# Turning q ahead of the last x tile, finishing its scalings a block earlier, and moving one tile's numerators behind a pair's second product

## The chip, the cores and the metric

The kernel runs on one core of one Trainium2 chip. The core's engines work side by side, each through its own list of instructions in a fixed order, and wait for one another through semaphores: PE (TensorE, matrix products; its weight loads are listed as PEld), DVE (VectorE), ACT (ScalarE), POOL (GpSimd) and SP (SyncE, which here only issues transfers; "SPq" in the profile is its queue). Transfers run on the core's 16 DMA engines. The metric is the device time of one execution in microseconds, less being better; several executions of each kernel are timed, and one more is recorded by the hardware profiler.

## The reference: what is computed

A linear attention (cosformer) over 8 batches, 8 heads, 576 positions and head size 64, and behind it a feed-forward block with a GELU gate over the 8·576 = 4608 tokens.

```python
theta = np.pi / 2.0 * pos / S
phi = lambda x: np.concatenate([np.maximum(x, 0) * cos_w, np.maximum(x, 0) * sin_w], axis=-1)
q_p, k_p = phi(q), phi(k)
kv  = np.einsum('bhsf,bhsd->bhfd', k_p, v)
z   = np.sum(k_p, axis=2)
num = np.einsum('bhsf,bhfd->bhsd', q_p, kv)
den = np.einsum('bhsf,bhf->bhs', q_p, z)[..., None] + 1e-06
attn_out = num / den                       # (8, 8, 576, 64)
x = attn_out.transpose(0, 2, 1, 3).reshape(4608, 512)
g = x @ w_gate                             # (4608, 1536)
gelu = 0.5 * g * (1.0 + erf(g / sqrt(2)))
out = (gelu * (x @ w_val)) @ w_out         # (4608, 512)
```

## The kernel before, in words

**Two sizes of work.** Attention goes by batch b (576 tokens, five tiles t = 0 to 4 of 128 tokens, the last one half used). The feed-forward part goes by block n of 512 tokens, nine blocks. The order of the instructions on every engine is the order of the Python calls; nothing is moved by a scheduler. While block n's feed-forward work runs, the attention of batch n+1 is made in between. The change touches blocks 3, 4 and 5.

**Attention of a batch.** q and k, staged in float32 (tile st), are scaled by cosine and sine tables and clipped at zero: `prep_both(b, part, j, engine)` does this for q and k together for one of nine position groups j, on ACT (line 192; "s8" is the sine part of group 8, "c8" the cosine part). When all 18 scalings of a batch are done, `turn_q(b)` issues two DMA transposes on SP (line 223, phis to qT). The tile qT has one buffer for all batches. `kv_unit(b)` makes the 72 small products of k and v (line 271). `nm_unit(b, t)` makes the numerators and denominators of one tile: eight products of qT with kv (line 312) into the PSUM banks 6 and 7, then three DVE instructions (lines 323 to 325: add, reciprocal, multiply) that leave x_sb. `turn_x(b, t)` turns x_sb into xT by one or two DMA transposes on SP (line 379); xT is what the feed-forward products read. x_sb has four buffers.

**Feed-forward from block 3 on.** The gate and value products of a pair of 128-wide column groups are made by seven half-size products instead of eight (class `Pair`, line 655, methods p1 to p7), with sums of weights made beforehand and sums of xT made by `x_sum` on POOL (line 635, T1 to T4 into tile fs). In blocks 3 to 5 there are five pairs for the column groups 0 to 9, and groups 10 and 11 are done by the plain `gv_unit` (line 431), one inside the third pair, one inside the fifth. The output products (line 548, `product`) are those of the block before, spread over the slots; their sums of hT are made on POOL (line 530) and their results collected on DVE (lines 561 and 566).

**The order.** `step(new, old, a, b, c)` interleaves one pair with attention: p1, p5, `a()`, p6, p2, `b()`, p3, and, where a plain unit follows, p7, the unit with `c()` in the middle, p4. a, b and c are slots: `slot(n, jt)` runs `o_step` (output products of block n-1, every third time a `flush` that puts stores on SP), then `attention(n, jt)`, then `more(n, jt)` (the x_sums of block n+1 are in slots 8 to 11). A pair's p7 and p4 are otherwise left to the pair behind it ("old"). The pairs of blocks 3 to 5 take the slots (0, 1), (2, 3), (4, 5, 6), (7, 8) and (9, 10, 11); the first and the fourth have no old pair. `numerators(n, jt)` decides by slot number which tile is made: the table in it maps a slot to a tile of batch n+1 (slot 0: the last tile of batch n). In the fourth pair it is called behind p1.

**Two waits inside a pair** matter here. p2 adds onto a copy of p1 that ACT makes (line 674); p3 adds onto bank MIX, which p6's DVE instruction writes (line 682), so PE cannot begin p3 before line 682 has ended on DVE, and DVE takes line 682 only behind the collecting of the output products of slot `a()` (lines 566 and 561).

**`attention(n, jt)`** first turns the x tiles whose numerators have been made since the last slot, then (slot 0, blocks 4 to 6) does the last two scalings s8 and c8 of batch n+1, then (slot 0, in block 3 slot 1) `turn_q(n+1)`, then `start_loads` (the loads of a later batch's q, k and v, on SP), then `kv_unit` in slot 1, and `preps` (the scalings of batch n+2 by the table PREPS).

Of the kernel before, what the change touches and what calls it, by code (L numbers as in the profile page):

```python
# [16 lines left out]
def kernel(  # L17
# [13 lines left out]
    nc = tc.nc  # L31
# [8 lines left out]
    R = S // 64  # L40
# [54 lines left out]
    def load(eng, name, b, m0, m1, j0=0, j1=R):  # L95
        if (name, b) not in staged:
            staged[name, b] = stage(name, b)
        eng.dma_start(
            out=staged[name, b][:, m0:m1, j0 * D:j1 * D],
            in_=rows(srcs[name], b)[:, m0:m1, j0 * D:j1 * D],  # L100
        )
# [64 lines left out]
    def phi_tile(name, b):  # L166
        phi[name, b] = phis[:, 1 if name == "k" else 2 * (b % 2) * (b > 2)]
        return phi[name, b]
# [15 lines left out]
    def prep_both(b, part, j, eng):  # L184
        for name in "qk":
            phi_tile(name, b)
        o = phis[:, b % 2:b % 2 + 2, :, j, part * D:(part + 1) * D]
        o = o.rearrange("p a m d -> p (a m) d")
        i = st[:, 0:2, :, j * D:(j + 1) * D].rearrange("p a m d -> p (a m) d")
        tab = (cos_t, sin_t)[part]  # L190
        if eng is nc.scalar:
            nc.scalar.activation(o, i, AF.Relu, scale=tab[:, j:j + 1])  # L192
        else:
            eng.tensor_scalar(o, i, 0.0, tab[:, j:j + 1], op0=ALU.max, op1=ALU.mult)  # L194
# [26 lines left out]
    def turn_q(b):  # L221
        for i in range(2):
            nc.sync.dma_start_transpose(
                out=qt_tile(b)[:, i].rearrange("f m (j p) -> f (m j) p", p=64),
                in_=phi["q", b][64 * i:64 * i + 64].rearrange("p m j f -> p (m j f)"),
            )
# [83 lines left out]
    def nm_unit(b, t, b0=6):  # L310
        for h in range(H):
            nc.tensor.matmul(  # L312
                bank(b0 + h // 4)[:, (h % 4) * (D + 1):(h % 4 + 1) * (D + 1)],
                lhsT=q_cols(b, t, h),
                rhs=kv_sb[b][:, h // 2, h % 2, :],
                start=True,
                stop=True,
            )
        nm = ps[:, b0:b0 + 2, 0:4 * (D + 1)].rearrange("p g (h d) -> p g h d", h=4)
        den = attn2.tile([128, 2, 4], FP32, name="den")  # L320
        rec = attn2.tile([128, 2, 4], FP32, name="rec")
        x = xsp.tile([128, 2, 4, D], BF16, name="x_sb")
        nc.vector.tensor_scalar_add(den, nm[:, :, :, D], EPS)
        nc.vector.reciprocal(rec, den)
        nc.vector.tensor_tensor(  # L325
            x,
            nm[:, :, :, 0:D],
            rec[:, :, :, None].to_broadcast([128, 2, 4, D]),
            op=ALU.mult,
        )  # L330
        xs[b, t] = x.rearrange("p g h d -> p (g h d)")
# [30 lines left out]
    def xT_block(blk):  # L362
        if blk not in xT:
            xT[blk] = xtp.tile([128, CT, BLK], BF16, name="xT")
        return xT[blk]

    def pieces(b, t):

        o = max(128 * (t + 1) - S, 0)
        c0, n = b * S + t * 128, 128 - o  # L370
        while n > 0:
            m = min(n, BLK - c0 % BLK)
            yield c0 // BLK, c0 % BLK, o, m
            c0, o, n = c0 + m, o + m, n - m

    def turn_x(b, t):
        x = xs.pop((b, t))
        for blk, c, o, m in pieces(b, t):
            nc.sync.dma_start_transpose(
                out=xT_block(blk)[:, :, c:c + m], in_=x[o:o + m, :]  # L380
            )
# [39 lines left out]
    def gv_unit(n, jt, c0=0, w=BLK, to=None, between=None):  # L421
        xt = xT[n]
        js = slice(jt * 128, (jt + 1) * 128)
        if to is None:
            to = (0, 1) if turn[0] % 2 == 0 else (2, 3)
            turn[0] += 1
        if n not in hT:
            hT[n] = ffn.tile([128, JT, BLK], BF16, name="hT")
        for g, wt in ((0, wg_sb), (1, wv_sb)):
            for ct in range(CT):  # L430
                nc.tensor.matmul(  # L431
                    bank(to[g])[:, 0:w],
                    lhsT=wt[:, ct, js],
                    rhs=xt[:, ct, c0:c0 + w],
                    start=(ct == 0),
                    stop=(ct == CT - 1),
                )
            if g == 0:
                gel = ffn.tile([128, BLK], FP32, name="gel")
                nc.scalar.activation(gel[:, 0:w], bank(to[0])[:, 0:w], AF.Gelu)  # L440
                if between:
                    between()
        nc.vector.tensor_mul(  # L443
            hT[n][:, jt, c0:c0 + w], gel[:, 0:w], bank(to[1])[:, 0:w]
        )
# [168 lines left out]
    def w_sum(name, j0, j1, eng=nc.vector):  # L614
        x, y, op = {
            "S1": ("A21", "A22", ALU.add),
            "S2": ("S1", "A11", ALU.subtract),
            "S3": ("A11", "A21", ALU.subtract),
            "S4": ("A12", "S2", ALU.subtract),
        }[name]  # L620
        eng.tensor_tensor(w_part(name, j0, j1), w_part(x, j0, j1), w_part(y, j0, j1), op=op)
# [83 lines left out]
    def step(new, old, a, b, c=None, std=None, to=None):  # L705

        n, (jt, *_) = new.n, new.at
        new.p1()
        if old:
            old.p7(6)  # L710
        elif n < 6:
            numerators(n, jt)
        new.p5()
        a()
        new.p6()
        if old:
            old.p4()
        new.p2()
        if n < 6 and old:
            numerators(n, jt + 1)  # L720
        b()
        new.p3()
        if std:
            new.p7(MIX)
            preps(n, f"m{std}")

            def between():
                numerators(n, jt + 2)
                c()
                new.p4()  # L730

            gv_unit(n, std, to=(to, to), between=between)
# [206 lines left out]
    def start_loads(n, jt):  # L939
        for b, name, *part in LOADS.get((n, jt), ()):  # L940
            if len(part) == 1:
                load(nc.sync, name, b, part[0], part[0] + 2)
            elif part:
                load(nc.sync, name, b, 0, NP, *part)
            else:
                for m in (0, 2):
                    load(nc.sync, name, b, m, m + 2)
# [63 lines left out]
    def early(jt):  # L1011
        for what in EARLY.get(jt, "").split():
            part = "cs".index(what[0])
            prep_both(4, part, int(what[1]), nc.scalar if part or jt > 8 else nc.gpsimd)

    def block2():
# [37 lines left out]

    PREPS = {
        2: "s0 c0", 4: "s1 c1", 5: "s2", "m10": "c2", 6: "s3 c3", 7: "s4 c4",
        9: "s5 c5", 10: "s6", "m11": "c6", 11: "s7 c7",
    }
    turns = []

    def preps(n, jt):
        b = n + 1
        if 3 < b < B - 1:
            for what in PREPS.get(jt, "").split():
                prep_both(b + 1, "cs".index(what[0]), int(what[1]), nc.scalar)

    def numerators(n, jt):
        b, t = n + 1, {6: 0, 7: 1, 10: 2, 11: 3, 0: 4}.get(jt)
        if jt == 0:
            b = n  # L1070
        if t is not None and b > 3:
            nm_unit(b, t)
            turns.append((b, t))

    def attention(n, jt):
        made = list(turns)
        if n > 5:
            if (n, jt) == (6, 0):
                numerators(n, jt)
            i, b = n * JT + jt - 6 * JT - 7, B - 1  # L1080
            if i in (0, 2, 4, 6, 8):
                nm_unit(b, i // 2)
                turns.append((b, i // 2))
        for bt in made:
            turn_x(*bt)
            turns.remove(bt)
        b = n + 1
        if (n, jt) == (3, 0):
            early(JT)
        elif jt == 0 and n < 7:  # L1090
            prep_both(n + 1, 1, R - 1, nc.scalar)
            prep_both(n + 1, 0, R - 1, nc.scalar)
        if n == 3 and 2 < jt < 7:
            w_sum(("S1", "S2", "S4", "S3")[jt - 3], WJ, WX, eng=nc.gpsimd)
        if jt == (n == 3) and b < B:
            turn_q(b)
        start_loads(n, jt)
        if b >= B:
            return
        if jt == 1:  # L1100
            kv_unit(b)
        preps(n, jt)
        if b + 1 < B and jt in (7, 8):
            m = 2 * (jt - 7)
            cast_v(b + 1, m, m + 2, nc.gpsimd.tensor_copy)
# [14 lines left out]
    old, places = None, (0, 1, 2)  # L1120
    for n in range(3, NB):
        jt = 0
        for T in range(JT // 2):
# [7 lines left out]
            jt = jts.stop  # L1131
            old, places = (None, (other, at, to)) if std else (new, (to, other, at))
# [55 lines left out]
```

## Time and profile before

| what | value |
|---|---|
| median of 3 runs | 308.31 us (308.21 to 309.02) |
| the profiled execution | 307.53 us, of which the span (first to last instruction) is 305.7 us |
| PE busy | 295.3 us, 97% of the span |
| PE weight loads | 228.8 us, 75% |
| DVE, ACT, POOL busy | 74%, 66%, 54% |
| granted TensorE clock | 0.996 of full speed |
| SP's transfers (queue q1) | 41.17 MB, 61.4% of the 16 DMA engines' span |
| blocks 3, 4 and 5 | 112.6 to 143.6, 143.6 to 175.3 and 175.3 to 205.9 us (from the first output product of each to that of the next) |

How to read it: an engine's busy share tells how little idle time there is to win; the timeline of PE shows where that idle time lies, as the distance between the end of one group of products and the start of the next; the chain of waits names what released PE at such a place; and the timeline of SP shows when each transfer was issued, since its queue takes them strictly one behind the other. Starts in a timeline are microseconds from the start of the span. Consecutive products overlap in the records, so the distance from start to start of the groups is what counts.

### The profile page before, as it was taken

To read this page: it belongs to the slowest core of one execution; us is meant where nothing else is said; L and a number is where in the kernel's file an instruction comes from. 1 tells how busy PE (TensorE), PEld (TensorE's weight loads), DVE (VectorE), ACT (ScalarE), POOL (GpSimd) and SP (SyncE) were. 2 spreads that over 40 slices of the span, in tenths; PEclk is the share of its full clock that TensorE was granted. 3 is DMA by queue.
4 is the path that set the end of the run, shared out by engine and by line. 5 is a ranking of instruction groups with operands and counts; after the bars stand their busy time and mean duration, and the time that the engine had idled before them with its cause. 6 is when DMAs were issued, how large, how long until landed. Compare 5 with 4: busy or idle time off the path is not lost.

```text
span 305.7 us, 8024 instructions
## 1 busy us (share of the span) xinstructions
PE 295.3 (97%) x3089; PEld 228.8 (75%) x3107; DVE 227.5 (74%) x496; ACT 202.1 (66%) x399; POOL 163.8 (54%) x140
## 2 busy tenths in 40 slices
PE   7899999999999999999999999999999999999993
PEld 3574456745786668787878788888898988888882
DVE  5866995998995765879676967796678785766772
ACT  7865592997572797878685878686655556555630
POOL 6585430000000989976935594579935965397310
PEclk9999999999999999999999999999999999999998
DMA  7999999989999989997799889937833521303045
GB/s 264 257 172 211 343 292 389 303 169 226 204 152 211 346 241 157 218 300 199 113 214 277 205 131 155 319 60 132 134 75 63 60 46 34 71 0 73 0 88 122
DMA packets 73175, 53.68 MB, mean 176 GB/s; under 512 B 45392, under 2 KB 62544, under 8 KB 73136
## 3 DMA queue, kind: packets, MB, share of 16 engines
q1 hardware_dynamic: 63360, 41.17, 61.4%
q0 software_dynamic: 9696, 11.93, 17.0%
q8 instruction: 24, 0.39, 0.5%
q14 instruction: 15, 0.12, 0.1%
q10 hardware_dynamic: 80, 0.07, 0.1%
HBM read 37.75 MB, written 9.44 MB: 154 GB/s over the span
## 4 chain that ended last, share of the span: by engine, by line
PE 77%; DMA 7%; DVE 6%; issue 5%; POOL 1%; ACT 1%; SPq 1%; POOLq 0%; DVEq 0%
PE ps L655 29%; PE ps L548 19%; PE ps L431 18%; PE ps L464 3%; PE ps L312 3%; DMA qT<-phis 3%; PE ps L271 3%; DMA st<-in_v_dram 2%; DMA wv_sb<-in_moe_w_val_dram 2%; DVE hT L443 1%; DVE phis L180 1%; POOL st L530 1%; PE ps L402 1%; PE ps L234 1%; DVE ps L682 1%
## 5 line engine op out<-in xcount | busy, mean ns | idle before, releaser
L530 POOL TENSOR_TENSOR sm<-hT 128x768 bf16<-128x768 bf16 x24 | 39.4, 1640 | 21.0 <-PE ps L655 8.0
L695 DVE TENSOR_TENSOR ps<-fs,ps 128x512 f32<-128x512 f32 x33 | 22.9, 695 | 27.7 <-PE ps L655 26.1
L431 PE MATMUL ps<-xT,wg_sb 128*128 128x512 bf16 (+1 forms) x172 | 41.3, 349 | 0.6
L431 PE MATMUL ps<-xT,wv_sb 128*128 128x512 bf16 (+1 forms) x182 | 41.8, 351 | 0.1
L655 PE MATMUL ps<-fs,ws 128*128 128x256 bf16 x288 | 40.8, 273 | 0.0
L655 PEld LDWEIGHTS <-ws 128*128 128x128 bf16 x384 | 36.3, 98 | 5.7 <-issue 0.7
L655 PE MATMUL ps<-xT,wg_sb 128*128 128x256 bf16 x264 | 39.6, 272 | 0.0
L194 POOL TENSOR_SCALAR phis<-st,cos_t 128x512 bf16<-128x512 f32 x4 | 7.9, 1984 | 54.8 <-PE ps L312 54.8
L443 DVE TENSOR_TENSOR hT<-gel,ps 128x512 bf16<-128x512 f32 (+1 forms) x46 | 28.0, 614 | 11.3 <-PE ps L431 8.6
L548 PEld LDWEIGHTS <-sm 128*128 128x128 bf16 x336 | 32.5, 98 | 4.5
L440 ACT ACTIVATE gel<-ps 128x512 f32<-128x512 f32 (+1 forms) x46 | 24.6, 541 | 15.8 <-PE ps L431 14.5
L548 PEld LDWEIGHTS <-hT 128*128 128x128 bf16 x288 | 28.0, 98 | 4.0 <-issue 0.2
L561 DVE TENSOR_TENSOR o_sb<-sm,ps 128x256 f32<-128x256 f32 x56 | 23.4, 417 | 10.1 <-ACT sm L566 8.9
L687 ACT ACTIVATE gel<-ps 128x512 f32<-128x512 f32 x33 | 19.6, 593 | 16.8 <-PE ps L655 16.7
L678 ACT COPY fs<-ps 128x512 f32<-128x512 f32 x33 | 19.3, 586 | 16.4 <-DVE ps L695 15.3
L655 PEld LDWEIGHTS <-wg_sb 128*128 128x128 bf16 x264 | 25.8, 98 | 4.7
L431 PEld LDWEIGHTS <-wv_sb 128*128 128x128 bf16 x184 | 17.9, 98 | 15.2 <-issue 0.3
L325 DVE TENSOR_TENSOR x_sb<-ps,rec 128x512 bf16<-128x512 f32 x38 | 26.3, 691 | 1.3
L530 POOL TENSOR_TENSOR sm<-hT,sm 128x768 bf16<-128x768 bf16 x12 | 19.7, 1639 | 11.9 <-PE ps L548 7.0
L192 ACT ACTIVATE phis<-st,sin_t 128x512 bf16<-128x512 f32 x36 | 25.7, 719 | 0.0
L431 PEld LDWEIGHTS <-wg_sb 128*128 128x128 bf16 x184 | 17.0, 98 | 11.4
L696 DVE TENSOR_TENSOR hT<-gel,ps 128x512 bf16<-128x512 f32 x33 | 22.7, 688 | 3.2
(134 smaller groups left out, 634.6 us busy)
## 6 DMA issues: line engine op xcount, KB each, us to landing
out_dram<-o_sb SPq DMA_DIRECT2D x69, 128.0 KB, 3.1
st<-in_v_dram SPq DMA_DIRECT2D x10, 576.0 KB, 7.5
st<-in_q_dram SPq DMA_DIRECT2D x5, 640.0 KB, 5.4
st<-in_q_dram SPq DMA_DIRECT2D x5, 512.0 KB, 5.7
st<-in_k_dram SPq DMA_DIRECT2D x4, 640.0 KB, 6.9
st<-in_k_dram SPq DMA_DIRECT2D x4, 576.0 KB, 4.6
st<-in_q_dram POOLq DMA_DIRECT2D x4, 576.0 KB, 12.0
st<-in_k_dram SPq DMA_DIRECT2D x4, 512.0 KB, 5.2
```

The costliest lines, as they stand in the source:

```text
L192: nc.scalar.activation(o, i, AF.Relu, scale=tab[:, j:j + 1])
L325: nc.vector.tensor_tensor(x, nm[:, :, :, 0:D], rec[:, :, :, None].to_broadcast([128, 2, 4, D]), op=ALU.mult,)
L431: nc.tensor.matmul(bank(to[g])[:, 0:w], lhsT=wt[:, ct, js], rhs=xt[:, ct, c0:c0 + w], start=(ct == 0), stop=(ct == CT - 1),)
L440: nc.scalar.activation(gel[:, 0:w], bank(to[0])[:, 0:w], AF.Gelu)
L443: nc.vector.tensor_mul(hT[n][:, jt, c0:c0 + w], gel[:, 0:w], bank(to[1])[:, 0:w])
L530: eng.tensor_tensor(a[name][:, j0:j1], a[x][:, j0:j1], a[y][:, j0:j1], op=op)
L548: nc.tensor.matmul(at, lhsT=hs.setdefault(key, h_parts(n, p))[a][:, j], rhs=ts[b][:, j], start=(j == 0 and i in ((1, 2, 4, 5), (1, 4, 5))[ ...
L561: nc.vector.tensor_tensor(o, got[key, k], x, op=op)
L655: nc.tensor.matmul(to[:, 256 * half:256 * half + 256], lhsT=w_part(a, j * 128, (j + 1) * 128)[:, ct], rhs=xb[self.n][b][:, ct], start=(hal ...
L687: nc.scalar.activation(self.gel0, self.other, AF.Gelu)
L695: nc.vector.tensor_tensor(bank(val), self.m5, self.sum, op=ALU.add)
L696: nc.vector.tensor_tensor(self.h(1), both(gel1), both(bank(val)), op=ALU.mult)
```

## The change

It has three parts, all in blocks 3 to 5 and the slots next to them. The numerators of tile 1 move, in the fourth pair, from behind p1 (slot number 7) to behind p2 (slot number 8); with them goes their turn_x, from slot 7 to slot 8, behind that slot's flush on SP. The scalings s8 and c8 of batches 5, 6 and 7 move from slot 0 of blocks 4, 5 and 6 to slot 11 of the blocks ahead, behind s7 and c7 on ACT. And in the slot of turn_q, turn_q and the loads that go with it are issued ahead of the x tile that was made since the last slot (tile 4 of batches 4 and 5), where they were issued behind it. No work is added or left out.

```diff
@@ step
         if old:
             old.p4()
         new.p2()
-        if n < 6 and old:
+        if n < 6:
             numerators(n, jt + 1)
         b()
         new.p3()
@@ PREPS
         2: "s0 c0", 4: "s1 c1", 5: "s2", "m10": "c2", 6: "s3 c3", 7: "s4 c4",
-        9: "s5 c5", 10: "s6", "m11": "c6", 11: "s7 c7",
+        9: "s5 c5", 10: "s6", "m11": "c6", 11: "s7 c7 s8 c8",
     }
@@ numerators
     def numerators(n, jt):
-        b, t = n + 1, {6: 0, 7: 1, 10: 2, 11: 3, 0: 4}.get(jt)
+        b, t = n + 1, {6: 0, 8: 1, 10: 2, 11: 3, 0: 4}.get(jt)
         if jt == 0:
             b = n
@@ attention
-        for bt in made:
-            turn_x(*bt)
-            turns.remove(bt)
         b = n + 1
         if (n, jt) == (3, 0):
             early(JT)
-        elif jt == 0 and n < 7:
-            prep_both(n + 1, 1, R - 1, nc.scalar)
-            prep_both(n + 1, 0, R - 1, nc.scalar)
         if n == 3 and 2 < jt < 7:
             w_sum(("S1", "S2", "S4", "S3")[jt - 3], WJ, WX, eng=nc.gpsimd)
         if jt == (n == 3) and b < B:
             turn_q(b)
-        start_loads(n, jt)
+            start_loads(n, jt)
+        for bt in made:
+            turn_x(*bt)
+            turns.remove(bt)
+        if jt != (n == 3):
+            start_loads(n, jt)
         if b >= B:
             return
```

## Prediction

> **What bounds the kernel now.** I read the page first: PE is busy 97% of the span, so only idle time of PE can be won, and no part of the change alters what PE computes. PE's list of waits over the whole span names one wait in blocks 3 to 5, and the chain of waits through block 4 (start us, length us, what) shows where it lies and a second place that the list does not name (first row the page's, the second that of the waits, then the chain):
>
> ```profile
> PE 295.3 (97%) x3089; PEld 228.8 (75%) x3107; DVE 227.5 (74%) x496; ACT 202.1 (66%) x399; POOL 163.8 (54%) x140
> ...
> PE ps L312 <- DMA qT<-phis: 0.7, 1, 0.7
> ...
> 150.51 8.54 DMA qT<-phis
> ...
> 159.10 0.40 PE ps L312 x7
> ...
> 163.93 0.43 DVE sm L566
> ...
> 164.73 0.70 DVE ps L682
> 165.43 0.04 issue
> 165.47 1.91 PE ps L655 x16
> ```
>
> So PE hung on the second transpose of q (line 223), and 6 us later on line 682. How long it stood is read from PE's timeline of block 4, start to start:
>
> ```profile
> 157.38 1.03 PE L431 MATMUL ps<-xT,wg_sb 128*128 128x512 bf16 x3
> 158.24 0.19 PE L312 MATMUL ps<-kv_sb,qT 128*128 128x65 bf16 x1
> 159.10 0.40 PE L312 MATMUL ps<-kv_sb,qT 128*128 128x65 bf16 x7 [0.67 <-DMA qT<-phis]
> 159.33 0.82 PE L548 MATMUL ps<-wo_sb,sm 128*128 128x256 bf16 x6
> ...
> 164.60 0.82 PE L548 MATMUL ps<-wo_sb,sm 128*128 128x256 bf16 x6
> 165.47 0.60 PE L655 MATMUL ps<-xT,ws 128*128 128x256 bf16 x4
> ```
>
> From line 431 to line 548 it is 159.33 − 157.38 = 1.95 us; the same stretch is 127.64 − 126.51 = 1.13 in block 3 and 190.20 − 189.07 = 1.13 in block 5. The wait for q costs 0.82 us, once. From that pair's second batch of output products to p3 it is 0.87, where six such products otherwise take 0.66: 0.21 us lost, and the same 0.87 stands in block 3 (132.90 to 133.77) and block 5 (195.46 to 196.33). SP's timeline shows why q came late: it issued two x transposes, then q without a pause, then the loads. The third row is the x tiles 0 and 1, the fourth the x_sum that waits for them:
>
> ```profile
> 144.02 2.58 SPq L379 DMA_TRANSPOSE xT<-x_sb  x2
> 146.71 7.90 SPq L223 DMA_TRANSPOSE qT<-phis  x2
> 154.66 1.60 SPq L98 DMA_DIRECT2D st<-in_q_dram  x1
> ...
> 161.47 4.36 SPq L379 DMA_TRANSPOSE xT<-x_sb  x3
> ...
> 167.79 1.16 POOL L635 TENSOR_TENSOR fs<-xT 128x512 bf16<-128x512 bf16 x1 [1.11 <-DMA xT<-x_sb]
> ```
>
> **Part 1, q ahead of the x tile (blocks 4 and 5), with s8 and c8 a slot earlier.** SP has turn_q issued at 146.71 because tile 4's transpose (half of 2.58: 1.29 us) is ahead of it. Without that, it can go at 144.02 + 1.29 = 145.31 if c8 is done. c8 began at 145.08 on ACT and would have ended at 145.8; in slot 11 it comes behind c7. ACT starts one scaling each 0.61 us: s7 140.82, c7 141.44, so s8 142.05, c8 142.66, ending 143.37. The last readers of the one qT buffer, tile 4's products, start at 142.78 and are over at 143.2. So q leaves 1.40 us earlier, bounded by its issue on SP. It landed at 159.05, 12.34 us after its first issue; the same 12.34 from 145.31 gives 157.65, and PE asks at 158.24. The wait goes with 0.59 us to spare: −0.82 us. Bounds: 0 (landing not moved) and −0.82. In block 5 q does not hold PE, so the same move is worth nothing there; in block 6 only c8 is earlier, also nothing.
>
> What the earlier scalings are put ahead of: ACT's copy of p1 (line 674), which began at 143.50 after 1.35 us of idle time waiting for DVE line 700. ACT is free again at 142.66 + 0.61 = 143.27, so it is not late; the same holds at 175.20 (1.36 idle) and 206.06 (1.35), for 2 × 0.61 = 1.22. If it were late by 0.2 us, p2 would hide it: it starts at 144.57, 0.5 us behind the copy's end. 0, bounds 0 and +0.1 a block.
>
> What q and the loads are put ahead of: tile 4's transpose, then four stores (158.97). SP's own order is only permuted, so from the stores on it stands where it stood. Tile 4 leaves at about 157.6 instead of 145.3, behind seven transfers. Its first reader is the x_sum at 167.79. The longest any x transpose took to land is 7.6 us (median 3.7): 165.2, before that. x_sb has four buffers, and tile 4's is written next as tile 3 of the next batch at 173.5. Hidden by some 2.6 us: 0. The loads go 1.4 us earlier into stages whose last readers are the moved scalings: 0.
>
> **Part 2, tile 1's numerators behind p2 (blocks 3, 4, 5).** The eight products take PE 0.26 us wherever they stand. Taken from behind p1 and put behind p2, they let p5, the output products of slot 7, p6 and p2 begin 0.26 earlier, and the output products of slot 8 begin when they did. DVE line 566 begins 0.02 us after the output products (163.91 in the chain), so lines 566, 561 and 682 follow them 0.26 earlier: 682 ends at 165.17 instead of 165.43. PE is ready for p3 at 164.60 + 0.66 = 165.26. The 0.21 us go, with 0.05 left; next late is PE itself. 3 × −0.21 = −0.63. Bounds −0.63 and 0: if line 561 or p6's products bound line 682 and not line 566, nothing is won.
>
> The three DVE instructions (0.20, 0.24 and 0.60 us from start to start: 1.04) leave the place ahead of line 566, where DVE then waited 0.62, and go behind line 682, ahead of line 695, where DVE waited 1.56 (166.98 in block 4). They fit: 165.07 to 166.3. Line 695 writes bank 6, which they read, and starts behind them anyway. 0.
>
> Behind them hangs tile 1's turn_x: x_sb ends at 166.3 instead of 163.3, and slot 8's two stores (1.22 us) now go ahead of it, into the time in which SP waits. In block 4 the tile is two transposes, issued at 166.35 and 167.55. X transposes issued around there landed in 3.4 to 5.9 us, median 4.3: 171.9. POOL, with 3.37 us idle before its next work, then makes T1 to T4, 1.24 and 3 × 1.11 us: T1 is there at 173.1, T2 at 174.2. Block 5 reads T1 in p5 at 174.74 − 0.21 = 174.53 and T2 in p6 at 175.62. Spare: 1.4 us. In block 3 it is one transpose: x_sb 134.5, landed 139.1 at that stretch's median of 4.5, T1 at 140.2, needed at 142.83; spare 2.6. Block 6 does not read batch 6's tile 1 at all. So 0, bounds 0 and +2.3 (third rival).
>
> **Where the trace and the Trainium skill differ.** The two q transposes move 2 × 590 kB (64 rows of 4608 two-byte values each) in 12.34 us: 96 GB/s. The Trainium skill ("DMA: Bandwidth & Descriptors", section "Latency and other measured facts") gives 261 GB/s as measured for DMA transposes in one kernel. By that figure, as an estimate, both would be through in 4.5 us, q would never have held PE, and only the 0.63 us would be left to win (307.7). The trace shows the wait, so the sum goes by the trace.
>
> **Sum.** −0.82 − 0.63 = −1.45, less a residue of 0.02 to 0.05 a block in part 2: −1.4 us. The profiled execution took 307.53 us (span 305.7), so 306.1 for one like it; it lay 0.78 below the median of the runs, so I forecast 308.31 − 1.4 = **306.9 us**, 0.45% less.
>
> **The rivals.**
> 1. The landing of q does not move. It is bound by what the DMA engines already carry (their share is 0.92 at 144 to 146 us and about 1 from 148 on), not by SP's issue. Against it: the share is 0.26 at 146 to 148, so q found them idle. The time: −0.63 alone, 307.7.
> 2. Line 682 does not come earlier, because p6's products or line 561 bound it. For it: the chain has 0.30 us of "issue" between lines 561 and 682. Against: that is pipelining on DVE, whose start spacing is the same everywhere. The time: −0.82 alone, 307.5. Both together: no change, 308.3.
> 3. The later x tile ends on the other side. Place: the first x_sum in slot 8 of blocks 3 and 4, and p5 of the next block's first pair behind it. It decides from a landing of 5.7 us in block 4 on. At the longest landing of the trace, 7.6 us from an issue at 167.55, T1 is there at 175.15 + 1.2 = 176.35 and PE waits 1.8 us; in block 3 134.55 + 7.6 + 1.2 = 143.35, 0.5 us. With the gains: −1.4 + 2.3 = +0.9, 309.2. For it: the stores now ahead of it, and landings that vary threefold. Against: the loads of block 4 are by then 1.4 us further on, and the landings beside them are below 6.
>
> **How the numbers follow.** A measurement of this kernel can tell about 0.3%, 0.9 us. Forecast 0.68 (its own range 306.3 to 307.4); rival 1 0.10, rival 2 0.09, both together 0.04, rival 3 0.09. The forecast lies 1.4 below and counts as faster, rivals 1 and 2 (0.6 and 0.8 below) mostly as same, with some of each as faster because the runs' own spread (0.8) reaches over the line, rival 3 as slower or same. Faster 0.74, same 0.18, slower 0.08. The range takes in rivals 1 and 2 and leaves out no change and rival 3: 306.2 to 308.0.
>
> **What would show it.** In the changed profile: no wait of PE line 312 for qT, and line 431 to line 548 at 1.13 in block 4; q's transposes issued directly behind one x transpose; 0.66 to 0.70 in place of 0.87 ahead of p3 in all three blocks; line 566 to 682 unchanged in spacing, lines 323 to 325 between 682 and 695; POOL's first line 635 of blocks 3 and 4 two to three us later, and no gap of PE at the first pair of blocks 4 and 5. The prediction is wrong if such a gap appears there, if q still lands after PE asks, or if ACT's line 674 starts late at the block's edge.

## The result, and the profile after

| | before | changed |
|---|---|---|
| median of 12 runs | 308.36 us | 306.14 us |
| lowest and highest | 307.29 to 309.94 | 305.41 to 308.49 |
| the profiled execution, and its span | 307.53, 305.7 | 305.74, 304.0 |

The ratio of the runs is 0.9927, with a 95% interval of 0.9905 to 0.9950: the change is worth 2.2 us (1.5 to 2.9). I had forecast 1.4 us, in a range from 306.2 to 308.0. The direction was right, the size too small, and the time lies 0.06 us below the range.

Of the two profiled executions alone, the forecast held. This is PE's timeline of the changed kernel in block 4 and at its two edges (start, length, engine, line, operands, count):

```profile
145.95 1.33 PE L271 MATMUL ps<-vx,phis 64*128 64x65 bf16 x72
...
156.91 1.03 PE L431 MATMUL ps<-xT,wg_sb 128*128 128x512 bf16 x3
157.78 0.42 PE L312 MATMUL ps<-kv_sb,qT 128*128 128x65 bf16 x8
158.03 0.82 PE L548 MATMUL ps<-wo_sb,sm 128*128 128x256 bf16 x6
...
163.04 0.42 PE L312 MATMUL ps<-kv_sb,qT 128*128 128x65 bf16 x8
163.30 0.82 PE L548 MATMUL ps<-wo_sb,sm 128*128 128x256 bf16 x6
163.96 0.60 PE L655 MATMUL ps<-xT,ws 128*128 128x256 bf16 x4
...
176.60 1.33 PE L271 MATMUL ps<-vx,phis 64*128 64x65 bf16 x72
```

From line 431 to line 548 it is now 1.12 us (1.95 before), so the wait for q is gone; from the second output products to p3 it is 0.66 (0.87 before), and 0.66 and 0.65 in blocks 3 and 5. From one block's products of k and v (line 271) to the next it is 30.65, 30.65 and 30.64 us, against 30.86, 31.71 and 30.85: 0.21, 1.06 and 0.21, together 1.48. That is the forecast's sum of 1.45, and nothing has come in its place. The other 0.25 us of the 1.7 by which the spans differ had arisen before block 3 (line 271 there at 115.30 and 115.55), where the two kernels are the same.

SP's timeline of the changed kernel, and below it ACT's, show the moved steps as forecast: q directly behind one x transpose, the loads behind it, then the last x tile; and c8 (ACT's first row) before the copy of p1 (line 674), which starts 2.91 us ahead of line 271 in both kernels:

```profile
143.56 1.28 SPq L379 DMA_TRANSPOSE xT<-x_sb  x1
144.95 8.04 SPq L223 DMA_TRANSPOSE qT<-phis  x2
153.03 1.44 SPq L98 DMA_DIRECT2D st<-in_q_dram  x1
...
157.08 1.20 SPq L379 DMA_TRANSPOSE xT<-x_sb  x1
```

```profile
142.20 0.71 ACT L192 ACTIVATE phis<-st,cos_t 128x512 bf16<-128x512 f32 x1
143.04 0.57 ACT L674 COPY ps<-ps 128x512 f32<-128x512 f32 x1
```

So the open question was not what the change does, but why the runs gave 2.2 us where one profile of each kernel adds up to 1.5. Theory A: the excess is the spread of the runs. Theory B: the wait for q varies from execution to execution, and the one profile of before that I had read caught a short one.

### The profile page after: what moved, and what is told of

Its sections match the earlier page's. It is cut to its first block, busy times and chain, and to the rows that moved or that the text cites. A ratio compares the mean times of both kernels' runs of the same rounds, so it can differ in the third digit from the quotient of the medians.

```text
span 304.0 us, 8032 instructions
## 1 busy us (share of the span) xinstructions
PE 294.7 (97%) x3089; PEld 228.8 (75%) x3107; DVE 226.7 (75%) x496; ACT 202.2 (67%) x399; POOL 165.9 (55%) x140
## 4 chain that ended last, share of the span: by engine, by line
PE 75%; DMA 8%; issue 5%; DVE 4%; POOL 3%; ACT 2%; SPq 1%; POOLq 0%; DVEq 0%; ACTq 0%
PE ps L655 32%; PE ps L548 19%; PE ps L431 14%; DMA st<-in_v_dram 5%; PE ps L464 3%; PE ps L271 3%; PE ps L312 2%; DMA wv_sb<-in_moe_w_val_dram 2%; DVE hT L443 2%; SPq L98 1%; POOL st L530 1%; DMA xT<-x_sb 1%; ACT phis L178 1%; PE ps L402 1%; POOL fs L635 1%
## 5 line engine op out<-in xcount | busy, mean ns | idle before, releaser
L443 DVE TENSOR_TENSOR hT<-gel,ps 128x512 bf16<-128x512 f32 (+1 forms) x46 | 28.0, 613 | 11.5 <-PE ps L431 8.8
## 6 DMA issues: line engine op xcount, KB each, us to landing
st<-in_q_dram POOLq DMA_DIRECT2D x4, 576.0 KB, 12.1
```

Of the source, the lines that this page charges most:

```text
L443: nc.vector.tensor_mul(hT[n][:, jt, c0:c0 + w], gel[:, 0:w], bank(to[1])[:, 0:w])
```

## The experiments

**The kernel before, again, and the changed kernel, again** (no edit).

> The kernel before, unchanged, as a control and for a second profile. The question: the runs gave the change 2.2 us where the waits of the two profiled executions add up to 1.45. Theory A (the waits read from one profile are the whole gain, the rest is the spread of the runs): ratio 1.000 within 0.2%, and the second profile has the same waits of PE in blocks 3 to 5: 0.82 for q in block 4, 0.21 ahead of p3 in each. Theory B (q's landing varies from execution to execution, and the first profile caught a short wait): the wait for q in block 4 differs by some tenths from 0.82, or one appears in block 5, where q landed only about 0.2 us before PE asked.

> The changed kernel, unchanged, as a second measure of the change. Theory A: the ratio moves toward 1 - 1.45/308.3 = 0.9953. Theory B: it stays near 0.993. Both: no wait of PE in blocks 3 to 5 in the profile.

Measured: 308.8 us, ratio 0.9993 (0.9975 to 1.0012), and 306.44 us, ratio 0.9919 (0.9892 to 0.9947). The changed kernel's profile has no wait for q. The second profile of before (span 308.0) has a wait twice as long as the first, at the same place in block 4:

```profile
158.76 1.03 PE L431 MATMUL ps<-xT,wg_sb 128*128 128x512 bf16 x3
159.63 0.19 PE L312 MATMUL ps<-kv_sb,qT 128*128 128x65 bf16 x1
161.45 0.40 PE L312 MATMUL ps<-kv_sb,qT 128*128 128x65 bf16 x7 [1.64 <-DMA qT<-phis]
161.69 0.82 PE L548 MATMUL ps<-wo_sb,sm 128*128 128x256 bf16 x6
```

161.69 − 158.76 = 2.93 us, 1.80 more than the undisturbed 1.13. A wait of 0.82 us in every execution, as theory A has it, falls with this row alone. The profile shows one more wait that varies: 0.95 us for an x_sum (line 635) at the edge of blocks 2 and 3, which is in neither kernel's changed part.

**Each half alone.**

```diff
@@ q_part_only, against the changed kernel
-        if n < 6:
+        if n < 6 and old:
...
-        b, t = n + 1, {6: 0, 8: 1, 10: 2, 11: 3, 0: 4}.get(jt)
+        b, t = n + 1, {6: 0, 7: 1, 10: 2, 11: 3, 0: 4}.get(jt)
@@ numerators_only, against the kernel before
-        if n < 6 and old:
+        if n < 6:
...
-        b, t = n + 1, {6: 0, 7: 1, 10: 2, 11: 3, 0: 4}.get(jt)
+        b, t = n + 1, {6: 0, 8: 1, 10: 2, 11: 3, 0: 4}.get(jt)
```

> The change without the move of the numerators: q ahead of the last x tile, s8 and c8 a block earlier. Theory A: -0.82 us, ratio 0.9973; the profile keeps 0.21 us ahead of p3 in blocks 3, 4 and 5 and has no wait for q. Theory B: -1.5 us or more, 0.995 or less, with the same profile.

> The move of tile 1's numerators alone. Both theories: -0.63 us, ratio 0.998; the profile has 0.66 in place of 0.87 ahead of p3 in the three blocks, and keeps the wait for q in block 4, which is longer than 0.82 or as long (q is issued with PE's earlier pace). If its ratio is 0.996 or less, the excess lies with the numerators and not with q.

Measured: q part 307.84 us, ratio 0.9965 (0.9944 to 0.9987); numerators 307.74, 0.9978 (0.9957 to 0.9998). The intervals are too wide (0.6 us either way) to tell the theories apart, but the profiles are not. The q part has no wait for q and keeps 0.86 ahead of p3 (133.37 to 134.23); the numerators alone have 0.65 there (164.98 to 165.63) and wait 1.61 us for q (lines 431 to 548: 2.74). In the profiles the halves do not touch each other: the 0.21 us is there or gone with the numerators, the wait for q with the order. The ratios of the halves add up to 1.8 us (1.1 for q, 0.7 for the numerators), where the whole change measured 2.2 and 2.5; with intervals this wide that is no contradiction, but it does not confirm the 2.2 either.

**Each half of the q part alone**: only the order on SP, and only the early scalings.

```diff
@@ order_only, against the kernel before (scalings_only is the change's PREPS line and its three removed lines of slot 0)
-        for bt in made:
-            turn_x(*bt)
-            turns.remove(bt)
         b = n + 1
...
             turn_q(b)
-        start_loads(n, jt)
+            start_loads(n, jt)
+        for bt in made:
+            turn_x(*bt)
+            turns.remove(bt)
+        if jt != (n == 3):
+            start_loads(n, jt)
```

> Only the order on SP: q and the loads ahead of the last x tile, s8 and c8 still in slot 0, numerators as before. c8 then ends about 1.1 us after the x tile of slot 11 has been issued, so q can leave only 0.8 to 0.9 us earlier than before instead of 1.4. Theory B (q's landing varies; the two profiles of before waited 0.82 and 1.8 us for it): the wait shrinks to 0 to 1.0 us, ratio 0.997 to 0.9985. Theory A (the wait is 0.82 everywhere): it is just gone, ratio 0.9973.

> Only s8 and c8 a block earlier, SP's order as before, numerators as before. q is issued behind the last x tile on SP in any case (there c8 had ended 0.9 us before q's issue), so both theories: the wait for q stays as long as in before (0.8 to 1.8 us), ratio 1.000 within 0.2%. If ACT's copy of p1 were late behind the scalings, PE would show a gap ahead of p2 at the edges of blocks 3/4, 4/5 and 5/6 and the ratio would be above 1.

Measured: order 307.34 us, ratio 0.9955 (0.9935 to 0.9976); scalings 308.22 us, ratio 1.0001 (0.9981 to 1.0021). With the order alone, c8 (145.80 on ACT) holds q until 146.55 and 0.14 us of wait is left in the profile, as expected. The ratio is below the numbers of both theories (1.4 us, with an interval from 0.7 to 2.0), so it does not decide between them. The early scalings alone win nothing: q stands behind the x tile on SP as before, and PE waits 1.67 us. So the order is the part that pays. That the scalings add to it is seen in the profiles only (q leaves at −1.00 us from line 271 with them and at −0.58 without); the runs do not show it, since the q part with both measured 1.1 us.

**No q to wait for.** Here `turn_q` is left out for batches 5 and 6.

```diff
-            turn_q(b)
+            if b in (5, 6):
+                qT[b] = qT[4]
+            else:
+                turn_q(b)
```

> The kernel before without the turning of q in batches 5 and 6 (four transposes and 2.4 MB less; those batches' numerators are made from batch 4's q, so their part of the output is not the reference's). Nothing in block 4 can wait for q, so the gain is the whole mean wait for q: theory A -0.82 us, ratio 0.9973; theory B -1.2 to -1.8 us, 0.994 to 0.996. The 0.21 us ahead of p3 stay in all three blocks.

Measured: 307.54 us, ratio 0.9961 (0.9942 to 0.9980): 1.2 us, between the theories' numbers, with an interval that takes in both.

**A third profile of the kernel before** was worth more than these ratios.

> The kernel before once more, for one more profile of it: the wait for q in block 4 is 0.8 to 1.9 us (so far 0.8 and 1.8, and 1.6 and 1.7 in two kernels with the same order on SP).

Its execution took 310.55 us, and its block 4 is 3.76 us longer than an undisturbed one (34.62 from line 271 to line 271, against 30.86). PE's timeline and, below it, the stretches of 1 us (stretch, length, busy time and count of PE, PEld, DVE, ACT, POOL; then the granted TensorE clock, the DMA share and GB/s):

```profile
157.61 1.03 PE L431 MATMUL ps<-xT,wg_sb 128*128 128x512 bf16 x3
...
160.59 0.40 PE L312 MATMUL ps<-kv_sb,qT 128*128 128x65 bf16 x7 [1.92 <-DMA qT<-phis]
160.82 1.20 PE L548 MATMUL ps<-wo_sb,sm 128*128 128x256 bf16 x6
...
165.15 0.60 PE L655 MATMUL ps<-fs,ws 128*128 128x256 bf16 x4
```

```profile
160.00:161.00 1.00, 0.41 (x9) 0.40 (x10) 0.00 (x0) 0.49 (x1) 0.00 (x0) 1.00 1.08 378
161.00:162.00 1.00, 1.00 (x7) 0.72 (x6) 0.91 (x3) 0.00 (x0) 0.00 (x0) 0.55 1.11 382
162.00:163.00 1.00, 1.00 (x6) 0.59 (x4) 0.57 (x3) 0.00 (x0) 0.83 (x1) 0.50 1.07 334
163.00:164.00 1.00, 1.00 (x4) 0.34 (x3) 0.60 (x1) 0.00 (x0) 0.81 (x1) 0.50 1.03 343
164.00:165.00 1.00, 1.00 (x10) 0.65 (x9) 0.31 (x1) 0.00 (x0) 0.00 (x0) 0.74 0.95 290
```

PE stood for 2.08 us, and behind the wait the granted clock fell to half for about 3.4 us: the stretch from line 548 to p5 took 165.15 − 160.82 = 4.33 us, where it took 2.65 in the first profile of before, 1.68 us more. So this wait for q was paid twice. The Trainium skill ("TensorE: Matmul & The Clock Gate", section "HAM oscillation — how this bites in real kernels") warns of idle gaps of PE above about 3.4 us; here an idle time of 1.92 us was enough, and one of 1.64 us (second profile) was not. Of the five profiles with the old order, this is the only one with the clock down behind the wait for q.

SP's timeline of this profile also shows where the wait came from:

```profile
144.25 3.92 SPq L379 DMA_TRANSPOSE xT<-x_sb  x2
148.28 7.98 SPq L223 DMA_TRANSPOSE qT<-phis  x2
```

The two x transposes held SP for 3.92 us instead of 2.58, with q behind them. The profiles with the old order side by side, times from line 271 of block 4, at which PE asks for q at 11.8:

| profile | q's first issue | q landed after it | PE lost |
|---|---|---|---|
| before, first | +0.30 | 12.34 | 0.82 |
| before, second | +0.29 | 13.32 | 1.80 |
| before, third | +1.63 | 12.26 | 2.08, and 1.68 by the clock |
| numerators only | +0.28 | 13.14 | 1.61 |
| scalings only | +1.34 | 12.14 | 1.67 |
| changed kernel, both profiles | −1.00, −0.99 | about 11.5, 12.6 | 0 |

With the old order, the sum of the first two numbers, less 11.8, is the loss within 0.03 us in each row. Both terms vary, by 1.3 and by 1.2 us. In the changed kernel the same sum is negative: about 1.3 and 0.2 us to spare. A landing as long as 13.32 would by the same sum still cost about 0.5 us there; no profile shows one.

**q behind the loads**, the opposite dose.

```diff
-            turn_q(b)
             start_loads(n, jt)
+            turn_q(b)
```

> The changed kernel with q put behind the loads of its slot, as the opposite dose: the loads take SP 3.8 to 4.2 us to issue, so q leaves that much later in block 4. If q's landing follows its issue, PE, which now has 0.3 to 1.4 us to spare, waits 2.5 to 4 us in block 4; if the loads' 2.2 MB also stand ahead of q in the DMA engines, 5 us or more. In block 5 the loads take 2 to 3 us, a wait of 1 to 3 us; in block 3 (q in slot 1) 2.1 us of issue and a wait of 0 to 2. If the landing is not bound by the issue (first rival), no wait at all.

Measured: 322.49 us in a single execution. q's first issue in block 4 went from −1.00 to +2.35, and PE waited as the table's sum has it: the landing took about 12.6 us, and 2.35 + 12.6 − 11.8 is 3.2. PE's list of waits, and the place in block 4:

```profile
PE ps L312 <- DMA qT<-phis: 11.2, 5, 4.1
```

```profile
163.57 1.03 PE L431 MATMUL ps<-xT,wg_sb 128*128 128x512 bf16 x3
165.18 0.20 PE L312 MATMUL ps<-kv_sb,qT 128*128 128x65 bf16 x1 [0.59 <-DMA qT<-phis]
167.62 0.56 PE L312 MATMUL ps<-kv_sb,qT 128*128 128x65 bf16 x7 [2.23 <-DMA qT<-phis]
167.99 1.47 PE L548 MATMUL ps<-wo_sb,sm 128*128 128x256 bf16 x6
```

167.99 − 163.57 − 1.13 = 3.29 us in block 4, within what was expected; 5.12 in block 3 and 3.92 in block 5, more than expected. The three blocks are 7.31, 4.50 and 5.60 us longer than in the changed kernel; I put the 5.1 us beyond the waits down to the clock again, which the profile has at 0.50 behind the waits in all three. My expectation had left that out.

**The x tile behind the loads**, the test of the third rival.

```diff
-        (3, 9): [(6, "q", 0, 5), (6, "k", 0, 5)],
+        (3, 8): [(6, "q", 0, 5), (6, "k", 0, 5)],
-        (4, 9): [(7, "q", 0, 5), (7, "k", 0, 5)],
+        (4, 8): [(7, "q", 0, 5), (7, "k", 0, 5)],
+        if jt != (n == 3):
+            start_loads(n, jt)
         for bt in made:
             turn_x(*bt)
             turns.remove(bt)
-        if jt != (n == 3):
-            start_loads(n, jt)
```

> The changed kernel with the two loads of slot 9 (640 KB each) of blocks 3 and 4 put into slot 8 ahead of tile 1's x transposes, so that they land late; the test of the third rival. In the changed kernel the first x_sum of slot 8 ended at 168.55 in block 4 and PE read it at 173.2, a spare of 4.7 us, and 139.4 against 142.6 in block 3, 3.2 us. If the loads (5 to 6 us to land) hold the x tile back by their whole landing, PE waits 0.5 to 2 us in the first pair of block 4 or 5 and the ratio goes to 0.995 to 1.000; if they only share with it, the spare covers it and the ratio stays at 0.992 to 0.993.

Measured: 307.57 us, ratio 0.9964 (0.9941 to 0.9986), on the losing side of the changed kernel's 0.9927. The first x_sum of block 4 on POOL, in the changed kernel and here, and p5 of block 5's first pair here:

```profile
167.39 1.16 POOL L635 TENSOR_TENSOR fs<-xT 128x512 bf16<-128x512 bf16 x1 [2.81 <-issue]
```

```profile
174.25 1.16 POOL L635 TENSOR_TENSOR fs<-xT 128x512 bf16<-128x512 bf16 x1 [8.59 <-DMA xT<-x_sb]
```

```profile
175.46 0.60 PE L655 MATMUL ps<-fs,ws 128*128 128x256 bf16 x4 [0.72 <-POOL fs L635]
```

In the changed kernel the sum starts 5.83 us ahead of p5 (173.22), 4.6 more than its own 1.24; put behind 1.3 MB of loads, it starts 1.21 ahead, and PE waits: that block's step is 31.66 us, 1.0 over 30.65. At the edge of blocks 3 and 4 the step stayed 30.65. The rival's mechanism exists, but it needs 4.6 us of lateness, which the change does not bring.

**Two attempts at a faster version.** The first puts the x tile of slot 11 behind q as well.

```diff
-        made = list(turns)
+        made = [] if jt == JT - 1 and n < 6 else list(turns)
```

> The changed kernel with the x tile of slot 11 (tile 3) also put behind q and the loads: q leaves 0.5 to 1.3 us earlier again. If some executions of the changed kernel still wait for q (its landing took 11.4 to 13.3 us in the profiles, and PE asks 12.8 us after the first issue), it is faster by up to 0.3 us and its runs spread less: ratio 0.991 to 0.993. If the changed kernel never waits, it is the same as that, 0.992 to 0.993.

Measured: 306.22 us, ratio 0.9928 (0.9902 to 0.9953). q left at −2.35 instead of −1.00, and nothing measurable was won; neither this profile nor the changed kernel's two have a wait for q.

The second aims at the x_sum wait at the edge of blocks 2 and 3 (0 to 0.95 us in the profiles so far).

```diff
-            if jt in (8, 9):
-                m = 2 * (jt - 8)
-                cast_v(4, m, m + 2, nc.gpsimd.tensor_copy)
+            if jt == 8:
+                cast_v(4, 0, 2, nc.gpsimd.tensor_copy)
             more(n, jt)
+            if jt == 9:
+                cast_v(4, 2, 4, nc.gpsimd.tensor_copy)
```

> The changed kernel with one more step, found in the profiles: at the edge of blocks 2 and 3 PE waited 0 to 1.0 us (0.95 in the second profile of before, 0.18 and 0.42 in others) for the second x_sum of block 3, ahead of which POOL makes the second half of the cast of v (1.15 us). Here that cast goes behind the second x_sum. Theory: the wait is gone in every execution, the mean of 0 to 1.0 us is won (0.2 to 0.5 us): ratio 0.990 to 0.992. If the cast then holds the 72 products of k and v at the start of block 3, PE waits ahead of line 271 and the ratio is that of the changed kernel or above.

Measured: 306.13 us, ratio 0.9928 (0.9908 to 0.9948). Its profile has no wait there (25.60 us from line 271 of block 2 to that of block 3), but other profiles have none either without this edit (25.61 in the first of before, 25.60 in order only), and the time cannot be told from the changed kernel's. Neither version beats it measurably.

## Why the prediction was wrong, point by point

- **q's wait, the term of 0.82 us: the step that failed.** The mechanism was right (issue on SP sets the landing, 12.3 us later; the order is what moves it; the early scalings let q leave the last 0.4 us earlier). The size was not: the five profiles with the old order lost 0.82, 1.80, 2.08, 1.61 and 1.67 us, 1.60 on average, and I had the smallest. I gave the wait the bounds 0 and −0.82, as if one execution's wait were its greatest. With 1.60 + 0.63 the sum is 2.2 us, the measured difference, but part of that agreement is luck. The runs that have the q part alone, the order alone or no q to turn put the term at 1.1, 1.4 and 1.2 us (0.4 to 1.7, 0.7 to 2.0, 0.6 to 1.8). And the stretch ahead of block 3, where the changed kernel is the kernel before, varies as much: line 271 of block 3 starts between 114.65 and 116.99 us in the 14 profiles. How much of the 2.2 us is q and how much is that stretch in the runs timed stays open. The landing was not the constant 12.34 us of my sum either: in the changed kernel it was about 11.5 and 12.6.
- **The clock behind a long wait was not in the sum at all.** The third profile of before shows it, 1.68 us in block 4. How often it happens in the timed runs stays open. They have only a mean clock over the whole span, and that does not tell the place. A mean of 0.991 or less occurs in 23 of 112 timed runs of kernels with the old order of q on SP, and in none of 77 with q ahead of the x tile or not turned at all. But the third profile itself has a mean of 0.993, and the one timed run at or below 0.991 of which there is a trace (scalings only, 0.990) has its half clock at 12 to 15 us, far ahead of block 4, and full clock behind its wait for q (rows as above):

```profile
12.00:13.00 1.00, 1.00 (x18) 0.80 (x18) 1.00 (x3) 0.56 (x2) 1.00 (x3) 0.50 0.40 63
13.00:14.00 1.00, 1.00 (x35) 0.90 (x30) 0.49 (x2) 0.23 (x3) 1.00 (x2) 0.50 1.10 126
...
162.00:163.00 1.00, 1.00 (x10) 0.80 (x9) 0.96 (x3) 0.00 (x0) 0.43 (x1) 1.00 1.12 385
```

The second profile of before has the same early stretch, and so have two kernels with the new order (order only, and tile 3 behind q). So the mean clocks cannot be counted for block 4.
- **The numerators, 0.63 us: right.** 0.87 became 0.65 or 0.66 in all three blocks and in every profile with this part; line 682 followed line 566, with the numerators behind it and ahead of line 695.
- **The terms set to 0: right.** Line 674 was not late (143.04, as far ahead of line 271 as before), the last x tile's transpose left at 157.08 without a reader waiting, and tile 1's x_sum had 4.6 us to spare in block 4, more than the 1.4 I had worked out. I had let it wait for the second of the tile's two transposes, but only the first belongs to block 5 (the other half of the tile is block 6's); it was issued at 164.92, landed in 2.3 us where I had taken 4.3, and the x_sum began at 167.39. One sign of the forecast did not come for this reason: POOL's first line 635 was to be two to three us later, and was 0.4 us earlier in block 4 and 1.6 later in block 3 (138.27 against 136.67).
- **The rivals.** The first (landing not moved by the issue) is refuted by both doses. The second (line 682 not earlier) is refuted by the numerators alone. The third needs 4.6 us more lateness than the change brings.
- **Theory A** (the wait is 0.82 us in every execution) is refuted by the profiles; the ratios alone, with 0.2% either way, could not have decided. That the spread of the runs has a share in the excess is not refuted.

## What to carry to other kernels

A wait for a transfer is a difference of two times that both vary; what one profile shows of it is a sample, not a bound. Before pricing its removal, profile the unchanged kernel two or three times and look at how its issue and its landing move; where engines run without gaps, the fixed waits (here 0.21 us on DVE) repeat to the hundredth while the transfers' waits do not. And a wait of the matrix engine can cost more than its length: in one of five profiles here, 1.92 us of idle time was followed by half the clock for 3.4 us. Whether a mean clock speaks of that wait is told only by a trace of where the clock was low.

## What the runs showed of the hardware that I had not expected

- An idle time of PE of 1.92 us in the middle of dense work was followed by about 3.4 us at a granted clock of 0.50, 1.68 us lost; one of 1.64 us was not.
- Idle time in shorter pieces was followed by it too. In four profiles (before second, scalings only, order only, tile 3 behind q) the clock is at 0.50 for about 3.4 us from 11 to 12 us on. Ahead of it, up to 11.2 us, lie three idle times of PE, the longest 0.90 to 1.34 us, together 1.81 to 2.16. At the same place, pieces that add up to 1.47 us (numerators only, q part) or 1.67 (x tile behind the loads) were not.
- The same pair of x transposes held SP's queue for 2.57 or 2.58 us in three profiles of the old order and for 3.92 and 3.63 us in two others; in these five the pair of q transposes of block 4 took 12.1 to 13.3 us from the first issue to the last landing.
